# One sigmoid for both score tiles of a visit, fixed PSUM banks in the runs of blocks, and one gate multiplication per block on GpSimd

## The chip, the core and the metric

The kernel runs on one core of one Trainium2 chip. The metric is the device time of one execution in microseconds (us), the median of several runs; lower is better. The engines of the core are named as in the profile: PE is TensorE (matmuls), PEld its weight loads, DVE VectorE, ACT ScalarE, POOL GpSimd, SP SyncE. POOL also issues the loads from device memory, SP the stores. PSUM, into which PE writes, has eight banks of 512 float32 columns on 128 partitions.

## What is computed

Sigmoid attention for 8 batches of 12 heads, then a gated two-layer network on its output, everything in float32 at the borders:

```
scores = q @ k.T / sqrt(64) - log(448)      # q, k, v: (8, 12, 448, 64)
attn   = sigmoid(scores) @ v                # heads side by side: x is (3584, 768)
h      = x @ w_in                           # (3584, 2048)
g      = h * sigmoid(beta * h)              # beta: (2048,)
out    = g @ w_out                          # (3584, 768)
```

## The kernel before

All matmuls take float16 operands and add up in float32 in PSUM. The order of the instructions on every engine is the order in which the Python code issues them; each engine works through its own queue in that order, and semaphores hold it where data or a buffer isn't ready.

**Groups and visits.** Four heads make a group `g`; three groups (QPB = 3) make a batch, so there are 24 groups. The 448 keys of a group are taken in four parts `jt`: three of 128 keys, and a last one of 64 keys. A *visit* `visit(g, jt)` (line 246) computes the scores of one part: eight matmuls (line 222; sixteen in the last part, which a visit does for two groups at once) into two *score tiles* of two PSUM banks each, and then `weigh` (line 233, the sigmoid on ACT at line 236) once for each tile, 128x896 values at a time, into a slot of `attns`. The slots (NAT = 14) are handed out by age from `at_free`. A later visit writes into the same two score tiles, so its matmuls wait until these sigmoids have read them. `attend(g)` (line 281) multiplies the weights of a whole group with v (line 292) into two further banks, and DVE casts these into `xT` (line 301).

**Fill.** Between the scores of two visits PE works on *units* of a list `fill`: single matmuls of the dense layers. First come units of the first layer (line 312, whose gate is a sigmoid on ACT at line 323 and a multiplication on DVE at line 326) and plain units of the second layer (line 341). From about a quarter of the kernel on, the second layer runs as `pairs` of token tiles in Strassen's form: seven products of ND = 8 units each (line 563) on sums of hidden tiles that DVE makes (line 552), with DVE and ACT adding the results up (lines 581 to 586). A product holds a PSUM bank (`held`) until its result is out. `single` (line 379) does a tile that has no partner. The loop at the end of the kernel sets the pace: with the estimates M1_US, M2_US for a unit and AV_US = 1.3 us for an `attend`, it spreads what is left of `fill` evenly over the visits that are left in the phase, and a visit that has an `attend` gets fewer units.

**Banks.** Score tiles have four of the eight banks while visits run (`share_psum(2)`); the other four go to whoever asks (`bank`), the one not held that was used longest ago first.

**Runs of blocks.** Three times (`first_layer`, batches 2 and 3, 4 and 5, 6 and 7) the visits stop, and the first layer of two batches runs as a Strassen product too: `blocks` (line 483), eight blocks `i` of seven products of three matmuls each (`product1`, line 465). A block ends in four results: A and D in banks where they are accumulated, B in its bank, and E, which DVE writes to SBUF (a slot of `attns`, line 525). Each gets its gate: a sigmoid on ACT (line 476) into one of three buffers `sg`, and a multiplication on DVE (line 479). ACT also makes the copies at lines 500 and 503, DVE the addition at line 511. The gates of E, D and B of a block are issued in the next block's round, so a ninth round ends the run. Eight units of `fill` are issued in the first round (two calls of `other()`, four units each) and four in the last round, between the last products 3 and 4. All eight banks serve the run; `bank` picks them by age, and A must get a bank whose last use had 448 columns. After it, `share_psum(2)` takes the four free banks used longest ago, in pairs, for the score tiles.

**Sums of weights.** Strassen's form needs sums of the weights, which DVE makes in halves of 128x1536 (`in_sum`, line 425, `weight_sum`, line 407). `some_sum` issues one after each visit, from visit (4, 2) on: S3, S2, S4, then T7, T6, T1, then T4 and T3 in place in `w_out`, and S1 in place in `w_in` once the first layer of batch 1 is issued.

Of the kernel before, what the change touches and what calls it, by code (L numbers as in the profile page):

```python
# [13 lines left out]
def kernel(  # L14
# [10 lines left out]
    nc = tc.nc  # L25
    AF = mybir.ActivationFunctionType
    ALU = mybir.AluOpType

    B, H, S, D = q.shape
# [11 lines left out]
    QPB = H // HQ  # L41
    NHC = DM // P
    NB1 = DFF // P // 2
# [5 lines left out]
    MSCALE = 1.0 / math.sqrt(D)  # L49
# [14 lines left out]
    used = dict.fromkeys(range(8), 0)  # L64
    scored = []
    held = {}

    psp = ctx.enter_context(tc.tile_pool(name="psp", bufs=1, space=bass.MemoryType.PSUM))
    ps = psp.tile([P, 8, 512], FP32, name="ps")
    n_sc = [0]  # L70
    width = [0] * 8

    def share_psum(sc: int, first: bool = False):

        age = min(used.values()) - 1 if first else max(used.values())
        while len(scored) > sc:
            used.update((i, age) for i in scored.pop())
        while len(scored) < sc:
            free = [i for i in used if i not in held.values()]
            scored.append(  # L80
                min(
                    ((i, i + 1) for i in free if i + 1 in free),
                    key=lambda two: sorted((used[i] for i in two), reverse=True),
                )
            )
            for i in scored[-1]:
                del used[i]

    def touch(i: int):
        used[i] = max(used.values()) + 1  # L90

    def bank(cols: int = S, hold=None, written: int = 0):
        i = min((i for i in used if i not in held.values() and width[i] >= written), key=used.get)
        touch(i)
        if hold is not None:
            held[hold] = i
        width[i] = cols
        return ps[:, i, 0:cols]

    nlogs = const.tile([P, 1], FP32, name="nlogs")  # L100
    dummy = const.tile([P, 1], FP32, name="dummy")
# [3 lines left out]
    NAT = 14  # L105
# [124 lines left out]

    places = {}

    def weigh(sco, n: int, places=()):
        slot = next((i for i in at_free if i in places), at_free[0])
        at_free.remove(slot)
        nc.scalar.activation(  # L236
            out=attns[:, slot, :, 0:n],
            in_=sco[:, :, 0:n],
            func=AF.Sigmoid,
            bias=nlogs[:, 0:1],  # L240
            scale=MSCALE,
        )
        return slot


    def visit(g: int, jt: int, also=()):
        if jt < JF:
            todo = [[s] for s in (2 * g, 2 * g + 1)]
        else:
            todo = [[2 * h, 2 * h + 1] for h in (g, *also)]  # L250
        todo = [(score_tile(), slots) for slots in todo]
        for e in range(PAIR):
            for sco, slots in todo:
                for s in slots:
                    for hh in range(2):
                        score(sco, 0, s, jt, hh, e, 0, S)
        for sco, slots in todo:
            slot = weigh(sco, S, places.get(g, ()))
            for s in slots:
                at_use(slot, (s, jt, 0), slice(0, S))  # L260

# [209 lines left out]
                skip_group_check=not start,  # L471
            )

    def gate(h, dc: int, b: int):
        sg = sigp.tile([P, S], FP32, tag="sg", name="sg")
        nc.scalar.activation(  # L476
            out=sg, in_=h, func=AF.Sigmoid, bias=0.0, scale=beta_sb[:, dc : dc + 1]
        )
        return lambda: nc.vector.tensor_tensor(  # L479
            out=gt[:, dc, b % 2 * S : b % 2 * S + S], in0=h, in1=sg, op=ALU.mult  # L480
        )

    def blocks(b: int, other):

        kept = {}

        def whole(key, i):
            h = kept.pop((i, key))
            if (i, key) in held:
                touch(held.pop((i, key)))  # L490
            half, second = {"A": (0, 0), "D": (0, 1), "B": (1, 0), "E": (1, 1)}[key]
            return gate(h, i + half * NB1, b + second)

        for i in range(NB1 + 1):
            p5 = scratch(6 + i % 2, 1).bitcast(FP32)
            if i < NB1:
                B = kept[i, "B"] = bank(S, (i, "B"))
                product1(b, i, 1, B, True)
                A = kept[i, "A"] = bank(S, (i, "A"), S)
                nc.scalar.copy(out=A, in_=B)  # L500
                D = kept[i, "D"] = bank(S, (i, "D"))
                product1(b, i, 5, D, True)
                nc.scalar.copy(out=p5, in_=D)
            if i:
                product1(b, i - 1, 3, kept[i - 1, "D"], False)
                late = whole("E", i - 1)
            else:
                other()
            if i < NB1:
                product1(b, i, 6, B, False)  # L510
                nc.vector.tensor_tensor(out=D, in0=B, in1=p5, op=ALU.add)  # L511
            if i:
                late()
                whole("D", i - 1)()
            if i < NB1:
                product1(b, i, 2, A, False)
                whole("A", i)()
            if i in (0, NB1):
                other()
            if i:  # L520
                product1(b, i - 1, 4, kept[i - 1, "B"], False)
            if i < NB1:
                product1(b, i, 7, B, False)
                E = kept[i, "E"] = scratch(8 + i % 2, 1).bitcast(FP32)
                nc.vector.tensor_tensor(out=E, in0=B, in1=p5, op=ALU.add)  # L525
# [142 lines left out]
    with tc.manual_schedule():  # L668
# [136 lines left out]
        def first_layer(b: int):  # L805
            while due:
                values(due.pop())
            while soon:
                soon.pop(0)()
            fill_units(len(fill) - at_fill[0] - ND)  # L810
            share_psum(0, True)
            fill.extend(window(b // 2))
            blocks(b, lambda: fill_units(ND // 2))

        for n, (g, jt, also) in enumerate(visits):
            now = lambda g=g, jt=jt, also=also: visit(g, jt, also)
            if jt == 0:
                if g + 2 < NQUAD and g + 2 not in raws:
                    load_qk(g + 2)
                if g + 1 < NQUAD and (g + 1) % QPB == 0:  # L820
                    load_v((g + 1) // QPB)
            if n in turn_at:
                first_layer(turn_at[n])
                share_psum(2)
# [63 lines left out]
```

## Time and profile before

| | |
|---|---|
| time, median of 3 runs (lowest to highest) | 384.84 us (384.68 to 384.84) |
| time of the profiled execution | 385.18 us |
| its span, first to last instruction | 383.4 us |
| PE busy | 374.5 us, 98% of the span |
| ACT busy | 268.4 us, 70% |
| DVE busy | 264.4 us, 69% |
| POOL busy | 67.5 us, 18% |

The span is some 1.8 us shorter than the time of the same execution; changes of the span are taken as changes of the time. The phases that matter: visits with units of the first layer up to about 102 us, visits with Strassen pairs at 104.7 to 133.4, 168.5 to 222.9 and 258.7 to 311.6 us, runs of blocks at 134.5 to 168.5, 224.5 to 258.7 and 313.1 to 347.3 us, and then units alone up to 380 us. A row of a timeline merges neighbours of one kind: start, length until the last of them ends, engine, line, names, count, and in brackets the idle time of the engine before it with what ended that. Matmuls overlap their successors by some 0.07 us in such a row.

### The profile page before, as it was taken

To read this page: it belongs to the slowest core of one execution; us is meant where nothing else is said; L and a number is where in the kernel's file an instruction comes from. 1 tells how busy PE (TensorE), PEld (TensorE's weight loads), DVE (VectorE), ACT (ScalarE), POOL (GpSimd) and SP (SyncE) were. 2 spreads that over 40 slices of the span, in tenths; PEclk is the share of its full clock that TensorE was granted. 3 is DMA by queue.
4 is the path that set the end of the run, shared out by engine and by line. 5 is a ranking of instruction groups with operands and counts; after the bars stand their busy time and mean duration, and the time that the engine had idled before them with its cause. 6 is when DMAs were issued, how large, how long until landed. Compare 5 with 4: busy or idle time off the path is not lost.

```text
span 383.4 us, 7441 instructions
## 1 busy us (share of the span) xinstructions
PE 374.5 (98%) x2927; PEld 187.1 (49%) x2927; DVE 264.4 (69%) x507; ACT 268.4 (70%) x376; POOL 67.5 (18%) x117
## 2 busy tenths in 40 slices
PE   8999999999999999999999999999999999999996
PEld 3467664443344455544444445544444455555663
DVE  3256465779795877886576667888667567889662
ACT  3987877699886758877778748878677747882000
POOL 8833343141141100013214100004100000000000
PEclk9999999999999999999999999999999999999999
DMA  8999999892249330009639431006803031000333
GB/s 116 178 193 203 197 204 199 197 120 50 50 59 192 52 82 0 2 1 120 135 54 212 74 89 41 2 0 91 139 25 84 0 84 41 2 1 3 82 82 125
DMA packets 42403, 34.31 MB, mean 89 GB/s; under 512 B 21872, under 2 KB 38912, under 8 KB 42368
## 3 DMA queue, kind: packets, MB, share of 16 engines
q0 software_dynamic: 36976, 22.81, 43.9%
q1 hardware_dynamic: 5392, 11.02, 9.8%
q8 instruction: 23, 0.38, 0.4%
q14 instruction: 12, 0.10, 0.1%
HBM read 45.62 MB, written 11.01 MB: 148 GB/s over the span
## 4 chain that ended last, share of the span: by engine, by line
PE 90%; DVE 5%; ACT 3%; issue 1%; ACTq 0%; DVEq 0%
PE ps L563 26%; PE ps L465 23%; PE ps L222 12%; PE ps L292 10%; PE ps L312 8%; PE ps L341 4%; PE ps L379 4%; PE ps L682 3%; ACT attns L236 2%; DVE gt L479 2%; DVE ps L511 1%; ACT sg L476 1%; ACT sg L323 1%; DVE gt L326 0%; DVE attns L525 0%
## 5 line engine op out<-in xcount | busy, mean ns | idle before, releaser
L236 ACT ACTIVATE attns<-ps,nlogs 128x896 f16<-128x896 f32 (+1 forms) x171 | 160.5, 991 | 48.1 <-PE ps L222 47.1
L222 PE MATMUL ps<-qT,kT 32*128 32x448 f16 (+3 forms) x864 | 56.6, 340 | 1.7 <-DVE gt L479 0.9
L563 PEld LDWEIGHTS <-sum 128*128 128x128 f16 x440 | 40.4, 98 | 35.7 <-issue 10.4
L476 ACT ACTIVATE sg<-ps,beta_sb 128x448 f32<-128x448 f32 x72 | 45.1, 630 | 7.9 <-PE ps L465 3.8
L465 PE MATMUL ps<-xT,w_S 128*128 128x448 f16 x216 | 48.7, 352 | 0.1
L465 PE MATMUL ps<-xT,w_in 128*128 128x448 f16 x216 | 48.7, 353 | 0.0
L563 PE MATMUL ps<-w_T,sum 128*128 128x384 f16 x264 | 48.7, 327 | 0.0
L301 DVE CAST xT<-ps 128x448 f16<-128x448 f32 (+1 forms) x54 | 28.6, 567 | 28.0 <-PE ps L292 27.7
L131 POOL DMA_DIRECT2D raw<-in_q_dram x27 | 14.9, 551 | 182.9 <-DVE kT L209 172.7
L479 DVE TENSOR_TENSOR gt<-ps,sg 128x448 f16<-128x448 f32 x72 | 42.4, 616 | 0.6 <-ACT sg L476 0.5
L312 PE MATMUL ps<-xT,w_in 128*128 128x224 f16 (+1 forms) x288 | 40.7, 291 | 1.3 <-ACT attns L236 0.8
L292 PE MATMUL ps<-attns,v 128*64 128x448 f16 (+3 forms) x432 | 41.3, 340 | 0.0
L465 PEld LDWEIGHTS <-w_in 128*128 128x128 f16 x288 | 28.0, 98 | 26.6 <-issue 1.1
L581 DVE TENSOR_TENSOR osb<-ps,osb 128x384 f32<-128x384 f32 x55 | 30.5, 554 | 15.1 <-PE ps L563 12.6
L552 DVE TENSOR_TENSOR sum<-gt 128x1024 f16<-128x1024 f16 x55 | 36.4, 680 | 0.2
L563 PE MATMUL ps<-w_out,gt 128*128 128x384 f16 x176 | 33.7, 327 | 0.5 <-DVE w_out L407 0.5
L312 PEld LDWEIGHTS <-w_in 128*128 128x128 f16 x288 | 26.3, 98 | 14.4 <-issue 7.1
L326 DVE TENSOR_TENSOR gt<-ps,sg 128x224 f16<-128x224 f32 (+1 forms) x48 | 21.2, 466 | 17.4 <-ACT sg L323 17.3
L563 PE MATMUL ps<-w_out,sum 128*128 128x384 f16 x176 | 32.3, 327 | 0.7 <-DVE sum L552 0.4
L222 PEld LDWEIGHTS <-kT 32*128 32x128 f16 (+1 forms) x864 | 15.6, 96 | 34.0 <-issue 27.9
L292 PEld LDWEIGHTS <-v 128*64 128x64 f16 (+1 forms) x432 | 18.9, 108 | 24.7 <-issue 17.3
L465 PEld LDWEIGHTS <-w_S 128*128 128x128 f16 x216 | 21.1, 98 | 19.9 <-issue 0.6
(48 smaller groups left out, 350.5 us busy)
## 6 DMA issues: line engine op xcount, KB each, us to landing
out_dram<-osb SPq DMA_DIRECT2D x98, 96.0 KB, 2.4
raw<-in_k_dram POOLq DMA_DIRECT2D x24, 224.0 KB, 5.6
raw<-in_q_dram POOLq DMA_DIRECT2D x21, 224.0 KB, 4.1
v<-in_v_dram POOLq DMA_DIRECT2D x32, 144.0 KB, 6.6
w_in<-in_moe_w_in_dram POOLq DMA_DIRECT2D x8, 384.0 KB, 10.5
w_out<-in_moe_w_out_dram POOLq DMA_DIRECT2D x4, 768.0 KB, 14.0
v<-in_v_dram POOLq DMA_DIRECT2D x16, 48.0 KB, 6.4
out_dram<-osb SPq DMA_DIRECT2D x2, 384.0 KB, 2.4
```

Source lines behind the costliest of these rows:

```text
L222: nc.tensor.matmul(sco[base : base + nk, hh, u0 : u0 + n], kT[g][lo : lo + BLK, jt * P : jt * P + nk, e], qT[g][lo : lo + BLK, c0 : c0 + n ...
L236: nc.scalar.activation(out=attns[:, slot, :, 0:n], in_=sco[:, :, 0:n], func=AF.Sigmoid, bias=nlogs[:, 0:1], scale=MSCALE,)
L292: nc.tensor.matmul(av[hh * D : (hh + 1) * D, 0:n], vs[b][base : base + nk, 2 * (s % NPAIR) + hh, jt], at[base : base + nk, hh, 0:n], start ...
L301: nc.vector.tensor_copy(out=xTs[b][:, s % NPAIR, c0 : c0 + n], in_=av[:, 0:n])
L312: nc.tensor.matmul(m1, w_in16[:, hc, dc * P : (dc + 1) * P], xTs[b][:, hc, c0 : c0 + n], start=(hc == 0), stop=(hc == NHC - 1),)
L326: nc.vector.tensor_tensor(out=gt[:, dc, off : off + n], in0=m1, in1=sg[:, 0:n], op=ALU.mult)
L465: nc.tensor.matmul(out, w[:, c, i * P : (i + 1) * P], m[:, c], start=(start and c == 0), stop=(c == KH - 1), skip_group_check=not start,)
L476: nc.scalar.activation(out=sg, in_=h, func=AF.Sigmoid, bias=0.0, scale=beta_sb[:, dc : dc + 1])
L479: return lambda: nc.vector.tensor_tensor(out=gt[:, dc, b % 2 * S : b % 2 * S + S], in0=h, in1=sg, op=ALU.mult)
L552: nc.vector.tensor_tensor(out=sums[t, i], in0=x, in1=y, op=op)
L563: nc.tensor.matmul(m2, (x if op is None else sums[t, i])[:, dc], w[:, dc], start=first, stop=(dc == ND - 1), skip_group_check=i >= 4,)
L581: nc.vector.tensor_tensor(out=out, in0=in0, in1=in1, op=op)
```

## The change

1. **One sigmoid a visit.** When a visit has two score tiles and the score tiles are banks 0 to 3, `weigh_two` replaces the two calls of `weigh`: one sigmoid over four banks, 128x1792 values, into two neighbouring slots of `attns`, taken as a pair. That is so in 73 visits; 19 sigmoids of 128x896 and the six of 2x224 in the early part stay. `share_psum` always gives the score tiles banks 0 to 3 (0 to 5 at the start).
2. **Fixed banks in a run of blocks.** B and D of block `i` take the pair `i % 3` out of banks 0 and 1, the two remaining "others", and banks 2 and 3; A takes one of two further banks by turns. A bank that a product still holds at the start goes to D of block 1.
3. **E's multiplication on GpSimd.** The gate multiplication of E (it reads SBUF alone) is issued to POOL's queue; those of A, B and D stay on DVE. In the built program an instruction that reloads POOL's library stands ahead of the first one. The gate of the last block's E is issued after all others.
4. **Units at the end of a run.** Instead of four units between the last products 3 and 4, there are two, and six more after the last product 4, ahead of the last E gate and of the next visit. Banks 0 to 3 are given back to the score tiles ahead of these units.
5. **Sums moved.** The sums S3, S2, S4 may start at the first visit with full tiles, (3, 0), and so the T sums move up too; S1 waits until 32 units of the first pairs are issued.
6. **Pace.** AV_US is 1.5 instead of 1.3, and the loop leaves 1.35 us of units instead of 2.0 us ahead of the first two runs. In the built program a visit with Strassen units now has mostly 11 or 12 of them where it had 11, and 2 where it had 3 beside an `attend`.

PE's instructions are the same in number and shape; only their order moves.

```diff
-    def share_psum(sc: int, first: bool = False):
+    def share_psum(sc: int):
+        scored[:] = [(2 * i, 2 * i + 1) for i in range(sc)]
+        last = max(used.values())
+        for i in range(2 * sc):
+            used.pop(i, None)
+        for i in range(2 * sc, 8):
+            used.setdefault(i, last)
...
+    def weigh_two(sco, places):
+        two = [i for i in range(0, NAT, 2) if i in at_free and i + 1 in at_free]
+        slot = min(two, key=lambda i: (i not in places, max(at_free.index(i), at_free.index(i + 1))))
+        at_free.remove(slot)
+        at_free.remove(slot + 1)
+        nc.scalar.activation(
+            out=attns[:, slot : slot + 2].rearrange("p n h s -> p (n h) s"),
+            in_=sco, func=AF.Sigmoid, bias=nlogs[:, 0:1], scale=MSCALE,
+        )
+        return slot, slot + 1
...
     def visit(g: int, jt: int, also=()):
-        for sco, slots in todo:
-            slot = weigh(sco, S, places.get(g, ()))
+        if len(todo) == 2 and len(scored) == 2:
+            ats = weigh_two(ps[:, 0:4, 0:S], places.get(g, ()))
+        else:
+            ats = [weigh(sco, S) for sco, _ in todo]
+        for slot, (_, slots) in zip(ats if n_sc[0] % 2 == 0 or len(todo) == 1 else ats[::-1], todo):
...
-    def gate(h, dc: int, b: int):
+    def gate(h, dc: int, b: int, engine):
-        return lambda: nc.vector.tensor_tensor(
+        return lambda: engine.tensor_tensor(
...
-    def blocks(b: int, other):
+    def blocks(b: int, other, scores: int):
+        rest = sorted(used, key=used.get)
+        firsts = [i for i in rest if width[i] == S and i not in held.values()][:2]
+        others = sorted((i for i in rest if i not in firsts), key=lambda i: i in held.values())
+        (b0, d0), (b2, d2) = scored
+        share_psum(0)
+        def take(key, i):
+            at = firsts[i % 2] if key == "A" else ((b0, d0), others, (b2, d2))[i % 3][key == "D"]
...
         def whole(key, i):
-            return gate(h, i + half * NB1, b + second)
+            return gate(h, i + half * NB1, b + second, nc.gpsimd if key == "E" else nc.vector)
...
             if i:
                 product1(b, i - 1, 3, kept[i - 1, "D"], False)
+            if 0 < i < NB1:
                 late = whole("E", i - 1)
...
-            if i in (0, NB1):
-                other()
+            if i == 0:
+                other(ND // 2)
+            if i == NB1:
+                share_psum(scores)
+                other(2)
             if i:
                 product1(b, i - 1, 4, kept[i - 1, "B"], False)
...
+        other(ND - 2)
+        whole("E", NB1 - 1)()
...
-        sums_todo += [(in_sum, n, p, L1E) for n in ("S1",) for p in range(2)]
+        sums_todo += [(in_sum, n, p, L1E + 4 * ND) for n in ("S1",) for p in range(2)]
...
-                if sums_todo and (g, jt) > (QPB + 1, 1) and at_fill[0] >= sums_todo[0][3]:
+                if sums_todo and at_fill[0] >= sums_todo[0][3] and (sums_todo[0][0] is in_sum or (g, jt) > (QPB + 1, 1)):
...
-        AV_US = 1.3
+        AV_US = 1.5
...
-            todo = left_us(L1B) if g < 2 * QPB else left_us(len(fill)) - (2.0 if g < 6 * QPB else 4.0)
+            todo = left_us(L1B) if g < 2 * QPB else left_us(len(fill)) - (1.35 if g < 6 * QPB else 4.0)
```

More of the change, by code (lines that the diff above doesn't have):

```diff
@@ L71, with bank @@
     width = [0] * 8
-    def share_psum(sc: int, first: bool = False):
[L75 to L87, printed above, removed]
-    def touch(i: int):
[L90 to L94, printed above, removed]
+    def share_psum(sc: int):
[5 more added lines that the diff above has]
+            used.setdefault(i, last)
+    def touch(i: int):
+        used[i] = max(used.values(), default=0) + 1
+    def bank(cols: int = S, hold=None, at=None):
+        if at is None:
+            at = min((i for i in used if i not in held.values()), key=used.get)
+        assert at not in held.values()
+        touch(at)
         if hold is not None:
-            held[hold] = i
-        width[i] = cols
-        return ps[:, i, 0:cols]
+            held[hold] = at
+        width[at] = cols
+        return ps[:, at, 0:cols]
     nlogs = const.tile([P, 1], FP32, name="nlogs")
@@ L231, with weigh @@
     places = {}
-    def weigh(sco, n: int, places=()):
-        slot = next((i for i in at_free if i in places), at_free[0])
-        at_free.remove(slot)
+    def weigh(sco, n: int):
+        slot = at_free.pop(0)
         nc.scalar.activation(
@@ L243, in weigh @@
         return slot
+    def weigh_two(sco, places):
[5 more added lines that the diff above has]
+            out=attns[:, slot : slot + 2].rearrange("p n h s -> p (n h) s"),
+            in_=sco,
+            func=AF.Sigmoid,
+            bias=nlogs[:, 0:1],
+            scale=MSCALE,
+        )
+        return slot, slot + 1
     def visit(g: int, jt: int, also=()):
@@ L496, in blocks @@
             if i < NB1:
-                B = kept[i, "B"] = bank(S, (i, "B"))
+                B = take("B", i)
                 product1(b, i, 1, B, True)
-                A = kept[i, "A"] = bank(S, (i, "A"), S)
+                A = take("A", i)
                 nc.scalar.copy(out=A, in_=B)
-                D = kept[i, "D"] = bank(S, (i, "D"))
+                D = take("D", i)
                 product1(b, i, 5, D, True)
@@ L511, in blocks @@
                 nc.vector.tensor_tensor(out=D, in0=B, in1=p5, op=ALU.add)
+            if 0 < i < NB1:
+                late()
             if i:
-                late()
                 whole("D", i - 1)()
@@ L517, in blocks @@
                 whole("A", i)()
-            if i in (0, NB1):
-                other()
+            if i == 0:
+                other(ND // 2)
+            if i == NB1:
+                share_psum(scores)
+                other(2)
             if i:
@@ L810, in first_layer @@
             fill_units(len(fill) - at_fill[0] - ND)
-            share_psum(0, True)
             fill.extend(window(b // 2))
-            blocks(b, lambda: fill_units(ND // 2))
+            blocks(b, fill_units, 2 if b < B - 2 else 0)
         for n, (g, jt, also) in enumerate(visits):
```

5 lines of the change are left out of this document (3 added, 2 removed).

## The prediction

> **What bounds the kernel now.** I read the page first, then what PE waited for, then stretches of PE's and ACT's timelines.
>
> ```profile
> span 383.4 us, 7441 instructions
> ...
> PE 374.5 (98%) x2927; PEld 187.1 (49%) x2927; DVE 264.4 (69%) x507; ACT 268.4 (70%) x376; POOL 67.5 (18%) x117
> ...
> PE 90%; DVE 5%; ACT 3%; issue 1%; ACTq 0%; DVEq 0%
> ```
>
> PE is busy for 98% and makes 90% of the chain that ended last. PE's instructions stay the same in number and shape, so the time can change only by what PE waits. The waits that the trace lists are short (us in total, times, longest):
>
> ```profile
> PE ps L222 <- DVE gt L479: 0.9, 1, 0.9
> ...
> PE ps L563 <- DVE w_out L407: 0.5, 1, 0.5
> PE ps L563 <- DVE sum L552: 0.4, 1, 0.4
> ```
>
> But a busy PE can hide a wait: a matmul that stands still behind another is drawn within one row. The visits show it; PE first, then ACT:
>
> ```profile
> 61.58 0.60 PE L222 MATMUL ps<-qT,kT 32*64 32x448 f16 x16
> ...
> 185.00 0.57 PE L222 MATMUL ps<-qT,kT 32*128 32x448 f16 x8
> ...
> 187.67 0.57 PE L222 MATMUL ps<-qT,kT 32*128 32x448 f16 x8
> 188.18 1.31 PE L563 MATMUL ps<-w_out,gt 128*128 128x384 f16 x7
> 189.33 0.81 PE L563 MATMUL ps<-w_out,sum 128*128 128x384 f16 x4
> 190.07 0.80 PE L222 MATMUL ps<-qT,kT 32*128 32x448 f16 x8
> ```
>
> ```profile
> 185.61 1.91 ACT L236 ACTIVATE attns<-ps,nlogs 128x896 f16<-128x896 f32 x2 [0.65 <-PE ps L222]
> ...
> 188.34 1.91 ACT L236 ACTIVATE attns<-ps,nlogs 128x896 f16<-128x896 f32 x2 [0.83 <-PE ps L222]
> ```
>
> The same eight score matmuls take 0.57 us or 0.80 us. The long one began 2.40 us after the visit before it, with 11 units between. ACT began 0.67 us after that visit (0.61 us after the one at 185.00), and its two sigmoids ended at 188.34 + 1.91 = 190.25. The visit at 190.07 wants to write the second score tile at once, loses 0.23 us, and so goes on at 190.30, 0.05 us after the sigmoid. So a visit followed by 11 units is bounded by the loop scores, two sigmoids, next scores. How much this takes in all, by the three phases with Strassen pairs (score line alone; stretch, length, PE busy with its matmuls, PEld busy, clock, DMA share, GB/s):
>
> ```profile
> 104.70:133.40 28.70, 7.18 (x96) 1.80 (x96) 1.00 0.64 101
> 168.50:222.90 54.40, 14.25 (x192) 3.60 (x192) 1.00 0.70 113
> 258.70:311.60 52.90, 13.54 (x184) 3.39 (x184) 1.00 0.42 77
> ```
>
> 472 matmuls are 45 visits of 8 and 7 of 16. Clean ones cost 45 x 0.57 + 7 x 0.60 = 29.9 us; PE spent 34.96 us. So 5.1 us of "busy" is standing still.
>
> **The change, part by part.** The sum is made against the profiled execution, 385.18 us; the median of the runs shown, 384.84 us, lies 0.34 us below, and I carry that difference over.
>
> *One sigmoid a visit.* The two lengths that the trace has:
>
> ```profile
> L236 ACT ACTIVATE attns<-ps,nlogs 128x896 f16<-128x896 f32 x165 | 157.4, 1004 | 48.1 <-PE ps L222 47.1
> ...
> L236 ACT ACTIVATE attns<-ps,nlogs 128x448 f16<-128x448 f32 x6 | 3.8, 635 | 0.0
> ```
>
> 448 columns more cost 1004 - 635 = 369 ns, so 1792 columns should take 1004 + 2 x 369 = 1742 ns, against the 1.91 us of the pair. The next scores may start 0.61 to 0.67 + 1.74 + 0.05 = 2.40 to 2.46 us after the last ones, and all four banks come free together, so the first matmul waits, not the third. What PE has in between: 2.40 us with 11 units, 2.56 us with 12 (a unit is 1.15 us / 7 = 0.164 us, from 188.18 to 189.33), and beside an `attend` 185.00 to 187.67 = 2.67 us with 3 units, hence 2.51 us with the 2 that it now gets. Only the visits with 11 units can still wait, by 0 to 0.06 us. By the changed order there are 26 of them; at 0.04 us that is 1.0 us. Of the 5.1 us, 0.74 us belong to the two visits counted next; 4.4 us less 1.0 us, less 0.2 us for the rounding of rows, gives **-3.2 us** (bounds -1.8 with 0.1 us left per visit, and -4.4).
>
> *The visits after a run of blocks.*
>
> ```profile
> 167.08 0.81 PE L563 MATMUL ps<-w_out,gt 128*128 128x384 f16 x4
> 167.89 0.73 PE L465 MATMUL ps<-attns,w_in 128*128 128x448 f16 x3
> 168.55 0.37 PE L222 MATMUL ps<-qT,kT 32*128 32x448 f16 x1
> 169.84 0.57 PE L222 MATMUL ps<-qT,kT 32*128 32x448 f16 x7 [0.93 <-DVE gt L479]
> ...
> 261.12 0.37 PE L222 MATMUL ps<-qT,kT 32*128 32x448 f16 x2
> 261.67 0.57 PE L222 MATMUL ps<-qT,kT 32*128 32x448 f16 x6 [0.17 <-ACT attns L236]
> ```
>
> After the first run the scores stand from 168.55 to 169.84, since the bank still waits for a late gate of the last block: 1.29 us. After the second they lose 0.55 us one visit later, since ACT is late. With fixed banks the last block uses none of banks 0 to 3: their last readers are the gates of block 6, which DVE finishes in the last round, and six more units (1.0 us) now stand before the scores, during which ACT does the last gates. I count both as gone, 1.84 us, and half of the 0.16 us that the last product 4 waits behind the four units in each of three runs (0.81 us for them instead of 4 x 0.164): **-2.1 us** (bounds -1.5 and -2.3). What is late next is the gate of B, wanted by the last unit of the second product, over 1 us later.
>
> *E's multiplication on POOL.* The run of blocks today, by window (length, then PE, PEld, DVE, ACT and POOL busy), then its rows on PE (one block apart), and on ACT, and the group of DVE's multiplication that moves:
>
> ```profile
> 134.50:168.50 34.00, 34.00 (x182) 17.51 (x180) 27.66 (x51) 26.12 (x46) 0.00 (x0) 1.00 0.10 24
> ```
>
> ```profile
> 143.81 1.30 PE L465 MATMUL ps<-xT,w_S 128*128 128x448 f16 x6
> ...
> 147.79 1.30 PE L465 MATMUL ps<-xT,w_S 128*128 128x448 f16 x6
> ```
>
> ```profile
> 143.45 0.52 ACT L500 COPY ps<-ps 128x448 f32<-128x448 f32 x1 [0.32 <-PE ps L465]
> ...
> 144.44 0.67 ACT L476 ACTIVATE sg<-attns,beta_sb 128x448 f32<-128x448 f32 x1
> 145.01 2.09 ACT L476 ACTIVATE sg<-ps,beta_sb 128x448 f32<-128x448 f32 x3
> ```
>
> ```profile
> L479 DVE TENSOR_TENSOR gt<-attns,sg 128x448 f16<-128x448 f32 x24 | 14.8, 617 | 0.8 <-ACT sg L476 0.8
> ```
>
> PE is busy without a gap, a block every 3.98 us; ACT (26.1 of 34 us) and DVE (27.7) have slack, POOL does nothing. So DVE's 0.62 us a block buys nothing inside a run. No row shows POOL multiplying. From below, it should not beat DVE's 0.617 us. From above, its length meets the three `sg` buffers: E, D, A and B take them in turn, so B's sigmoid needs the buffer that POOL reads for E. E's sigmoid ends at 145.11, B's begins at 145.01 + 2.09 - 0.63 = 146.47 (0.63 us being one sigmoid): POOL has 1.36 us, and with ACT's idle 0.32 us about 1.7 us, before a block takes longer. I take **0** and need not choose a value below that. By the Trainium skill (GPSIMD Engine Reference, "Performance versus the Vector engine"), a tensor_tensor add of 2048 columns takes 4497 ns on GpSimd and 2293 ns on VectorE, 1.96 times; from that page I would estimate 1.21 us here, and the sum stays the same; no run so far shows it.
>
> *POOL's queue.* The loads issued behind the multiplications now wait for them.
>
> ```profile
> 128.24 0.54 POOL L131 DMA_DIRECT2D raw<-in_k_dram  x1
> 171.23 0.53 POOL L131 DMA_DIRECT2D raw<-in_q_dram  x1 [42.45 <-DVE kT L209]
> ```
>
> POOL already stands through the run, waiting for DVE's transposes after it. One pair of loads that went early (at 127.72) now goes after the run; its group is transposed six visits (some 15 us) later. **0**, and the reload ahead of the first multiplication has the idle time since 128.8.
>
> *The sums of weights.* T3 now ends long before its product: the 0.5 us on L407 go, **-0.5 us**. In exchange S sums of 0.93 us stand in DVE's queue earlier:
>
> ```profile
> L425 DVE TENSOR_TENSOR w_S<-w_in,w_S 128x1536 f16<-128x1536 f16 x4 | 3.7, 926 | 0.0
> ```
>
> ```profile
> 51.86 0.20 DVE L209 STREAM_TRANSPOSE kT<-raw 128x64 f32<-128x64 f32 x1
> ...
> 53.14 0.57 PE L222 MATMUL ps<-qT,kT 32*128 32x448 f16 x8
> ```
>
> One half comes just before the chain of copies and transposes of which this is the last, whose end (52.06) the scores at 53.14 need. 1.08 us of slack less 0.93 us, less what the gates ahead of it may be late: **+0.4 us** with the `attend` behind it (bounds 0 and 0.93).
>
> *The start and end of a run.* Ahead of the first run six units (1.0 us) less now stand between the last `attend` and product 1, while DVE still makes that product's input sums: **+0.3 us** (0 to 0.6). D of block 1 takes the bank that the last product held: **+0.1 us**. After the last run the wait for the sum on L552 goes, as DVE is 0.6 us ahead: **-0.4 us**.
>
> Sum: -3.2 - 2.1 - 0.5 + 0.4 + 0.3 + 0.1 - 0.4 = -5.4 us; 385.18 - 5.4 - 0.34 = **379.4 us**. With all bounds taken together it reaches from 376.8 to 383.5 us.
>
> **Rivals.**
> 1. *The wait changes its name.* All four banks come free at once, and a slot pair may be late too. If the new sigmoid takes the 1.9 us of the old two, the first matmul of a visit waits as long as the third did: the 3.2 us are gone, 382.6 us, up to 384.0 with the other terms poor. For it: PE needs all four banks, and 11 units leave no slack. Against: the slope of two rows.
> 2. *The first multiplication is late.* If the library is loaded only when the first one starts, ACT stands behind its `sg` buffer, and what it is late beyond 1.7 us is lost, once: 5 us late would give 382.7 us. Against: POOL has 12 us of idle time ahead. By the Trainium skill (GPSIMD Engine Reference, "Instruction dispatch"), the first call after a load of the library pays about 6 us; nothing in this trace shows it.
> 3. *POOL is too slow.* Each us beyond 1.7 us is paid in some 22 blocks. From 2.0 us on the kernel is slower than before: 22 x 0.3 = 6.6 us eat the gain; at 2.5 us it takes 397 us. For it: no row of POOL's arithmetic. Against: that would be over three times DVE's time.
> 4. *POOL and DVE take turns* on SBUF. DVE's five other operations of a block (3 x 616 + 632 + 615 ns, the means of the rows below) make 3.1 us; with t for POOL a block would take 3.1 + t. Beyond t = 0.9 us each block grows; from t = 1.15 us the kernel is slower (22 x 0.28 us), and 1.2 us gives 386.5 us.
>
> ```profile
> L479 DVE TENSOR_TENSOR gt<-ps,sg 128x448 f16<-128x448 f32 x72 | 42.4, 616 | 0.6 <-ACT sg L476 0.5
> ...
> L511 DVE TENSOR_TENSOR ps<-ps,attns 128x448 f32<-128x448 f32 x24 | 15.2, 632 | 16.9 <-PE ps L465 15.4 <-ACT sg L476 1.5
> L525 DVE TENSOR_TENSOR attns<-ps,attns 128x448 f32<-128x448 f32 x24 | 14.8, 615 | 0.0
> ```
>
> Against: these rows read one side from PSUM (`ps`). By the Trainium skill (SBUF — State Buffer, "Who interferes with whom"), a VectorE instruction with two SBUF inputs blocks, and is blocked by, a GpSimd instruction that reads SBUF, for its whole length; one with a single SBUF input isn't. By that rule the turns come only at a run's end, where the last E meets a `sum`, some 0.1 to 0.7 us.
>
> **How the numbers follow.** The sum 0.58; rival 1 0.17; rival 2 0.07; rival 3 0.05; rival 4 0.08; better than all bounds, 0.05. The range 376.8 to 384.0 us holds the first three, 0.82. A measurement can tell about 0.2% from no change, 0.77 us. Faster by more: 0.84 (the sum, rival 2, most of rival 1, the better case). Within: 0.04. Slower by more: 0.12.
>
> **What would show it.** Visits: ACT rows of 1.74 us, score rows of 0.57 us nearly everywhere, PE's time on the score line near 31 us in the three phases. Runs: PE without a gap inside, POOL rows under 1.36 us, no wait of ACT on POOL. Ends: scores that follow six units without a wait on a gate. It would be wrong if PE waits for ACT at most visits, or a block takes more than 3.98 us.

## The result, and the profile after

| | before | after |
|---|---|---|
| median (lowest to highest, runs) | 384.76 us (384.55 to 384.84, 4) | 381.15 us (380.91 to 381.19, 4) |
| profiled execution, its span | 385.18, 383.4 us | 381.19, 379.4 us |

The ratio is 0.9906, 95% interval 0.9889 to 0.9923: 3.6 us faster by the medians, 4.0 us by the two profiled executions, against the 5.4 us of the sum. The page of the changed kernel (span, busy time of each engine, shares of the chain that ended last, and the two groups that are new):

```profile
span 379.4 us, 7379 instructions
...
PE 370.7 (98%) x2927; PEld 186.2 (49%) x2927; DVE 256.8 (68%) x483; ACT 258.4 (68%) x303; POOL 94.7 (25%) x141
...
PE 91%; DVE 5%; ACT 3%; issue 1%; ACTq 0%
...
L245 ACT ACTIVATE attns<-ps,nlogs 128x1792 f16<-128x1792 f32 x73 | 128.0, 1753 | 49.3 <-PE ps L217 49.1
L491 POOL TENSOR_TENSOR gt<-attns,sg 128x448 f16<-128x448 f32 x24 | 27.3, 1137 | 151.3 <-ACT sg L488 151.3
```

The one sigmoid takes 1.753 us (1.742 reckoned) and GpSimd's multiplication 1.137 us. PE still bounds the kernel. The score line in the three phases with Strassen pairs (stretch, length, PE busy with its matmuls):

```profile
104.70:133.00 28.30, 6.35 (x96) 1.62 (x96) 1.00 0.54 86
167.00:222.00 55.00, 12.17 (x192) 3.08 (x192) 1.00 0.73 119
255.50:307.00 51.50, 11.58 (x184) 3.37 (x184) 1.00 0.46 81
```

30.1 us in place of 35.0: the standing still inside the visits is gone. Some of it has only moved. PE's timeline, then ACT's:

```profile
266.30 0.57 PE L217 MATMUL ps<-qT,kT 32*128 32x448 f16 x8
266.81 1.96 PE L593 MATMUL ps<-w_T,sum 128*128 128x384 f16 x11
268.79 0.58 PE L217 MATMUL ps<-qT,kT 32*128 32x448 f16 x8
...
271.22 0.58 PE L217 MATMUL ps<-qT,kT 32*128 32x448 f16 x8
```

```profile
266.99 1.75 ACT L245 ACTIVATE attns<-ps,nlogs 128x1792 f16<-128x1792 f32 x1 [0.82 <-PE ps L217]
269.42 1.75 ACT L245 ACTIVATE attns<-ps,nlogs 128x1792 f16<-128x1792 f32 x1 [0.68 <-PE ps L217]
```

The sigmoid ends at 266.99 + 1.75 = 268.74 and the scores start 0.05 us later, at 268.79. The next ones start at 271.22, which is 269.42 + 1.75 + 0.05. No row shows a wait: PE's rows lie end to end, and the standing still shows only in the distance between starts, which is 2.40 us for 11 units where nothing waits. Over the 25 visits with 11 units and no `attend` (the first at 104.96, the last at 298.71) the score matmul comes 0 to 0.11 us late, 1.5 us in all, and the one visit with ten units (130.53) 0.25 us. In all, 24 of the 52 visits of these phases still come more than 0.02 us late.

The waits that the view of PE's waits lists (total, times, longest) have a new first entry among the products (line 593):

```profile
PE ps L593 <- DVE sum L582: 1.1, 3, 0.8
...
PE ps L593 <- DVE xT L313: 0.4, 1, 0.4
...
PE ps L217 <- DVE kT L200: 0.2, 1, 0.2
```

Before, PE waited for a `sum` once and 0.4 us; now it does three times, each time behind a run of blocks. The timeline of all engines there, first run:

```profile
167.72 0.58 PE L217 MATMUL ps<-qT,kT 32*128 32x448 f16 x8
168.11 1.13 POOL L491 TENSOR_TENSOR gt<-attns,sg 128x448 f16<-128x448 f32 x1 [3.31 <-ACT sg L488]
168.17 1.62 DVE L582 TENSOR_TENSOR sum<-gt 128x1024 f16<-128x1024 f16 x1
168.22 1.47 PE L593 MATMUL ps<-w_out,gt 128*128 128x384 f16 x8
...
169.85 0.66 PE L593 MATMUL ps<-w_out,sum 128*128 128x384 f16 x3 [0.15 <-DVE sum L582]
```

The scores start at 167.72 with no wait on a gate, as forecast. But the `sum` takes 1.62 us where its like takes 0.68, and it ends 0.55 us after POOL's multiplication (168.11 + 1.13 = 169.24). By the distances between matmul starts PE loses 0.31, 0.32 and 0.93 us at the three ends. At the last end PE had stood for a `sum` before too; the rows of the kernel before, then of the changed one:

```profile
349.20 1.90 DVE L552 TENSOR_TENSOR sum<-gt 128x1024 f16<-128x1024 f16 x3
349.95 2.29 PE L563 MATMUL ps<-w_out,sum 128*128 128x384 f16 x13 [0.39 <-DVE sum L552]
```

```profile
344.23 1.13 POOL L491 TENSOR_TENSOR gt<-attns,sg 128x448 f16<-128x448 f32 x1 [3.30 <-ACT sg L488]
344.28 2.82 DVE L582 TENSOR_TENSOR sum<-gt 128x1024 f16<-128x1024 f16 x3
345.96 2.77 PE L593 MATMUL ps<-w_out,sum 128*128 128x384 f16 x16 [0.76 <-DVE sum L582]
```

### The profile page after: what moved, and what is told of

It is laid out like the page before. It is cut to its first block, busy times and chain, and to the rows that moved or that the text cites. A ratio compares the mean times of both kernels' runs of the same rounds, so it can differ in the third digit from the quotient of the medians.

```text
span 379.4 us, 7379 instructions
## 1 busy us (share of the span) xinstructions
PE 370.7 (98%) x2927; PEld 186.2 (49%) x2927; DVE 256.8 (68%) x483; ACT 258.4 (68%) x303; POOL 94.7 (25%) x141
## 4 chain that ended last, share of the span: by engine, by line
PE 91%; DVE 5%; ACT 3%; issue 1%; ACTq 0%
PE ps L477 25%; PE ps L593 25%; PE ps L217 12%; PE ps L304 10%; PE ps L324 9%; PE ps L353 4%; PE ps L391 4%; PE ps L712 3%; DVE sum L582 1%; ACT attns L230 1%; DVE xT L313 1%; ACT sg L488 1%; DVE ps L535 1%; DVE w_S L437 1%; DVE gt L491 1%
## 5 line engine op out<-in xcount | busy, mean ns | idle before, releaser
L245 ACT ACTIVATE attns<-ps,nlogs 128x1792 f16<-128x1792 f32 x73 | 128.0, 1753 | 49.3 <-PE ps L217 49.1
L491 POOL TENSOR_TENSOR gt<-attns,sg 128x448 f16<-128x448 f32 x24 | 27.3, 1137 | 151.3 <-ACT sg L488 151.3
L217 PE MATMUL ps<-qT,kT 32*128 32x448 f16 (+3 forms) x864 | 51.8, 340 | 1.3 <-ACT attns L230 0.6
L491 DVE TENSOR_TENSOR gt<-ps,sg 128x448 f16<-128x448 f32 x72 | 44.6, 619 | 1.4 <-ACT sg L488 1.0
L582 DVE TENSOR_TENSOR sum<-gt 128x1024 f16<-128x1024 f16 x55 | 38.9, 729 | 0.2
L535 DVE TENSOR_TENSOR ps<-ps,attns 128x448 f32<-128x448 f32 x24 | 15.2, 632 | 24.4 <-PE ps L477 24.4
```

The source lines that it names most:

```text
L217: nc.tensor.matmul(sco[base : base + nk, hh, u0 : u0 + n], kT[g][lo : lo + BLK, jt * P : jt * P + nk, e], qT[g][lo : lo + BLK, c0 : c0 + n ...
L245: nc.scalar.activation(out=attns[:, slot : slot + 2].rearrange("p n h s -> p (n h) s"), in_=sco, func=AF.Sigmoid, bias=nlogs[:, 0:1], scal ...
L491: return lambda: engine.tensor_tensor(out=gt[:, dc, b % 2 * S : b % 2 * S + S], in0=h, in1=sg, op=ALU.mult)
L582: nc.vector.tensor_tensor(out=sums[t, i], in0=x, in1=y, op=op)
```

## The experiments

All of them are edits of the changed kernel. Chips differ a little, so each was timed beside the kernel before on its own chip; PE's stalls are read from the profiles.

| kernel | median us | before, same chip | ratio (95% interval) | span |
|---|---|---|---|---|
| lastE_dve | 379.18 | 385.18 | 0.9846 (0.9832 to 0.9859) | 377.9 |
| lastE_early | 379.90 | 385.18 | 0.9865 (0.9851 to 0.9878) | 377.5 |
| allE_dve | 380.55 | 385.18 | 0.9883 (0.9870 to 0.9897) | 378.5 |
| two_sigmoids | 383.42 | 385.18 | 0.9955 (0.9943 to 0.9968) | 381.3 |
| pool_twice | 392.59 | 385.10 | 1.0195 (1.0179 to 1.0210) | 390.7 |
| pool_twice_sg4 | 381.22 | 385.10 | 0.9903 (0.9888 to 0.9918) | 379.5 |
| combo2 | 379.19 | 385.10 | 0.9849 (0.9835 to 0.9864) | 377.4 |
| combo3 | 379.34 | 385.10 | 0.9854 (0.9837 to 0.9870) | 377.6 |
| no_units | 380.81 | 384.87 | 0.9892 (0.9877 to 0.9907) | 379.3 |
| banks_shared | 384.82 | 384.87 | 0.9997 (0.9988 to 1.0006) | 382.7 |
| banks_no_units | 386.99 | 384.87 | 1.0055 (1.0042 to 1.0069) | 385.5 |
| av_13 | 383.58 | 384.87 | 0.9964 (0.9952 to 0.9977) | 381.8 |

**Why the sums are late: lastE_dve and lastE_early.** The theory was that VectorE and GpSimd take turns where both have only SBUF operands; the rival, that the sums are late for another reason.

```diff
-            return gate(h, i + half * NB1, b + second, nc.gpsimd if key == "E" else nc.vector)
+            return gate(h, i + half * NB1, b + second, nc.gpsimd if key == "E" and i < NB1 - 1 else nc.vector)
```

> The changed kernel with the last block's E multiplication of each run on VectorE; the other 21 stay on GpSimd. In the changed kernel the sum behind a run takes 1.62 us instead of 0.68 (168.17) while POOL multiplies (168.11 to 169.24), and PE waits 0.31, 0.32 and 0.93 us for these sums. Theory (VectorE and GpSimd take turns when both have only SBUF operands): the sums take 0.6 to 0.7 us again, all three waits go, 381.15 - 1.5 = 379.6 us. Rival (the sums are late because VectorE is late after the last gates, and 1.62 us is a wait on something else): E's 0.62 us on VectorE make them later still, 381.2 to 382.5 us.

lastE_early keeps the multiplication on GpSimd, earlier:

```diff
-            if 0 < i < NB1:
+            if i:
                 late = whole("E", i - 1)
...
-            if 0 < i < NB1:
+            if i:
                 late()
...
-        whole("E", NB1 - 1)()
```

> The changed kernel with the last E kept on GpSimd but issued as in the other blocks, ahead of D's gate, so that POOL multiplies from about 166.7 to 167.9, before the first sum behind the run. Theory (turns): the sum is short again, though it starts up to 0.6 us later since D's and B's sigmoids stand behind E's; the waits of 0.31 and 0.32 us go and 0.93 falls to about 0.4: 380.0 us. Rival (the sum is slow behind a run whatever POOL does): the sum still takes 1.6 us and starts later, 381.8 to 383 us.

The timeline of lastE_dve, then of lastE_early, behind the first run:

```profile
168.23 0.69 DVE L582 TENSOR_TENSOR sum<-gt 128x1024 f16<-128x1024 f16 x1
...
168.84 0.62 DVE L491 TENSOR_TENSOR gt<-attns,sg 128x448 f16<-128x448 f32 x1
```

```profile
166.08 1.14 POOL L491 TENSOR_TENSOR gt<-attns,sg 128x448 f16<-128x448 f32 x1 [2.06 <-ACT sg L488]
166.56 1.16 DVE L491 TENSOR_TENSOR gt<-ps,sg 128x448 f16<-128x448 f32 x2 [0.79 <-ACT sg L488]
...
167.74 0.69 DVE L581 TENSOR_TENSOR sum<-gt 128x1024 f16<-128x1024 f16 x1
```

In both the `sum` takes 0.69 us. lastE_dve adds E's 0.62 us to VectorE and still loses all three waits; its span is 1.5 us shorter, as expected. lastE_early leaves the work on GpSimd and only ends it before the sums: two of the waits go and the third falls from 0.93 to 0.36 us. So the rival falls: what stretches the `sum` is GpSimd's instruction beside it. VectorE's instructions that read PSUM are not stretched: in the rows of lastE_early the first of two gates starts beside POOL, and both take 1.16 us together; in the runs of blocks of the changed kernel the 21 gates that overlap a multiplication take 0.614 us on average, the others 0.620 us. That is the rule of the Trainium skill that the prediction cited (SBUF — State Buffer, "Who interferes with whom"), and here the traces agree with it on both sides. The sums differ from the gates also in type (f16) and width, which no run separates from the place of their inputs.

**What GpSimd is worth inside a run: allE_dve.**

```diff
-            return gate(h, i + half * NB1, b + second, nc.gpsimd if key == "E" else nc.vector)
+            return gate(h, i + half * NB1, b + second, nc.vector)
```

> The changed kernel with all 24 E multiplications on VectorE. Theory of the prediction (inside a run GpSimd buys nothing, since VectorE has 3.1 + 0.62 = 3.7 of 3.98 us to do in a block): the same time as with only the last E on VectorE, within 0.3 us, and blocks stay at 3.98 us. Rival (VectorE at 93% of a block is late for its gates): blocks grow by up to 0.1 us, 2 us in all, over the kernel with only the last E moved.

It is 1.4 us slower than lastE_dve, so the theory's "within 0.3 us" fell. But no block is longer: from the 13th to the 164th of a run's 168 product matmuls both take 28.56 us. The time is lost at the last block alone, as PE's waits and the timeline of allE_dve show:

```profile
PE ps L477 <- DVE attns L553: 1.0, 3, 0.3
```

```profile
165.07 0.49 PE L593 MATMUL ps<-w_out,gt 128*128 128x384 f16 x2
165.21 0.61 DVE L553 TENSOR_TENSOR attns<-ps,attns 128x448 f32<-128x448 f32 x1
...
165.87 0.73 PE L477 MATMUL ps<-attns,w_in 128*128 128x448 f16 x3 [0.32 <-DVE attns L553]
```

The last product 4 needs the bank that L553 reads; with E's multiplication of the block before ahead of it on VectorE, L553 is late for a product that has only two units before it. From its first product matmul to its last a run takes 33.94 us instead of 33.51: 0.43 x 3 = 1.3 us.

**The price of GpSimd: pool_twice and pool_twice_sg4.**

```diff
-        return lambda: engine.tensor_tensor(
...
+        def multiply():
+            for _ in range(2 if engine is nc.gpsimd else 1):
+                engine.tensor_tensor(
+                    out=gt[:, dc, b % 2 * S : b % 2 * S + S], in0=h, in1=sg, op=ALU.mult
+                )
...
```

> The changed kernel with every E multiplication done twice on GpSimd, into the same place, so 2.27 us a block there instead of 1.14. Theory of the prediction (the third sigmoid after E's needs the sg buffer that POOL reads; 1.36 us are free, 1.7 with ACT's idle time): blocks grow from 3.98 us to about 4.55, ACT waits for POOL, 22 x 0.57 = 12.5 us in the runs, and 3 x 1.1 us more at their ends, where the sums wait for both multiplications: 381.15 + 16 = 397 us. Rival (GpSimd has the whole block, since the slack of the gates takes it up): blocks stay at 3.98 us, only the ends pay, 384.5 us.

pool_twice_sg4 adds:

```diff
-    sigp = ctx.enter_context(tc.tile_pool(name="sigp", bufs=3))
+    sigp = ctx.enter_context(tc.tile_pool(name="sigp", bufs=4))
...
-        still = const.tile([P, 512], FP16, name="still")
+        still = gt[:, NDC - 1, 0:512]
+        beta_in = gt[0:BLK, NDC - 2, 0 : 2 * P].bitcast(FP32)
```

> The same with four sg buffers instead of three (idle weights and the input of beta lie in gt to make room). Theory (the buffer is what bounds, not GpSimd): blocks are back at 3.98 us though POOL works 2.27 us in each, only the ends pay, about 384.5 us. Rival (GpSimd's work itself, or turns with VectorE inside the block, bounds): as slow as with three buffers.

ACT and POOL in pool_twice, and ACT's row among its waits:

```profile
153.10 1.16 ACT L488 ACTIVATE sg<-ps,beta_sb 128x448 f32<-128x448 f32 x2
155.67 0.63 ACT L488 ACTIVATE sg<-ps,beta_sb 128x448 f32<-128x448 f32 x1 [1.42 <-POOL gt L493]
```

```profile
153.28 2.35 POOL L493 TENSOR_TENSOR gt<-attns,sg 128x448 f16<-128x448 f32 x2 [2.20 <-ACT sg L488]
```

```profile
ACT sg L488 <- POOL gt L493: 29.0, 21, 1.4
```

B's sigmoid starts at 155.67, when POOL has ended (153.28 + 2.35 = 155.63). In each run PE stands five times for 0.58 to 0.59 us and once for 0.34: blocks of 4.56 us, against 4.55 reckoned. With a fourth buffer all of that is gone, 381.22 us. So the forecast's limit is the buffer, not the engine. The total came out lower than expected, since six blocks a run pay and not seven, and since the `sum` at each end comes only 0.45 us later than in the changed kernel in pool_twice and no later in pool_twice_sg4, where 1.1 us had been expected in both (a later product of the last end loses 0.23 us in both). POOL and VectorE of pool_twice_sg4 (its lines shift a little):

```profile
167.79 2.67 POOL L492 TENSOR_TENSOR gt<-attns,sg 128x448 f16<-128x448 f32 x2 [2.14 <-ACT sg L487]
```

```profile
167.85 1.62 DVE L585 TENSOR_TENSOR sum<-gt 128x1024 f16<-128x1024 f16 x1
```

The `sum` still takes 1.62 us: it goes between the two multiplications, and these take 2.67 us in place of 2.35. Here turns are taken by instruction, at each of the three ends.

**The visits: two_sigmoids and av_13.** two_sigmoids weighs each tile by itself again, on the same banks and slots:

```diff
-            ats = weigh_two(ps[:, 0:4, 0:S], places.get(g, ()))
+            two = [i for i in range(0, NAT, 2) if i in at_free and i + 1 in at_free]
...
+            ats = [weigh(sco, S) for sco, _ in (todo if n_sc[0] % 2 == 0 else todo)]
...
-        for slot, (_, slots) in zip(ats if n_sc[0] % 2 == 0 or len(todo) == 1 else ats[::-1], todo):
+        for slot, (_, slots) in zip(ats, todo):
```

> The changed kernel with two sigmoids of 896 columns a visit again, on the same banks and slots. Theory (loop of scores, sigmoid, next scores): sigmoids take 2 x 1.0 us less overlap, 1.91 us instead of 1.75, the visits' waits rise from some 1.8 us to about 4.1 us, 383.5 us (1 to 5 us more than 381.15). Rival 1 of the prediction (the wait only changed its name): 381.2 us within 0.5.

It costs 1.9 us by the spans and 2.3 us by the medians (383.42 against 381.15 us), and the standing still is back inside the visits: 3.9 us there, where the changed kernel has 1.8 us ahead of them. Its timeline, PE then ACT:

```profile
277.55 0.78 PE L217 MATMUL ps<-qT,kT 32*128 32x448 f16 x8
```

```profile
275.81 1.91 ACT L230 ACTIVATE attns<-ps,nlogs 128x896 f16<-128x896 f32 x2 [0.70 <-PE ps L217]
```

The theory holds, and rival 1 of the prediction falls, though it is right in part: of the old 4.1 us, 1.8 only changed their place.

```diff
-        AV_US = 1.5
+        AV_US = 1.3
```

> The changed kernel with an attend reckoned at 1.3 us as before instead of 1.5. Visits beside an attend get 3 units again and others 11 instead of 12, some 10. Theory (the loop of 2.49 us bounds every visit of 11 units, 2.40 us, and every one of 10, 2.24 us, while 3 units beside an attend leave 0.2 us unused): the visits wait 1.0 to 1.5 us more, 382.4 us. Rival (the units are the same in number, so it matters little where they stand): 381.15 us within 0.3.

2.4 us slower by the span, twice the theory's. In the three phases 31 visits now have 11 units and five have ten, and those of ten lose 0.25 us each, four of them new; with the further visits of 11 units the visits wait 1.3 us more, as the theory said. The rest it had not seen: 0.99 us at 52.01, where a product of the second layer waits for its gate, less the 0.26 us that stood at that place, and 0.45 us at 292.65, where an `attend` comes just before a product that opens a bank.

**The scores after a run: no_units, banks_shared, banks_no_units.** All three have lastE_dve's edit. no_units takes away the eight units; banks_shared puts B and D of the last block into score banks; banks_no_units does both:

```diff
-                other(2)
...
-        other(ND - 2)
```

```diff
-            at = firsts[i % 2] if key == "A" else ((b0, d0), others, (b2, d2))[i % 3][key == "D"]
+            at = firsts[i % 2] if key == "A" else ((b0, d0), others, (b2, d2))[2 if i == NB1 - 1 else i % 3][key == "D"]
...
+        share_psum(scores)
         other(ND - 2)
```

> The changed kernel with the last E of each run on VectorE (379.2 us), and without the eight units of the second layer between the last block's products and the next scores; the units go to the later visits. Theory (the fixed banks alone took away the wait of the scores on a gate; the units only gave ACT time): the first scores after a run start at once, with no wait on a gate, and the second visit waits 0.5 to 0.7 us since ACT's first sigmoid stands behind those of B and E; in exchange 16 visits get 12 units instead of 11 and wait 0.09 us less: about 379 us, within 0.8. Rival (the units are what covers the gates): the first scores wait about 1.3 us as in the kernel before, 381 to 382 us.

> The changed kernel with the last E of each run on VectorE, and with B and D of the last block in two of the four score banks (2 and 3) instead of in two others; the eight units stay. Theory: the third score matmul after a run waits for B's gate, which ends 0.42 us after these scores start (168.19 against 167.77): 0.45 us in each of two runs, 380.1 us. Rival (six units are cover enough): no wait, 379.2 us.

> Both together: B and D of the last block in score banks, and no units between them and the scores. Theory (the fixed banks and the units each cover the gates; without both it is the wait of the kernel before): the first visit after a run stands 1.2 to 1.5 us until B's gate, twice, 2 to 3 us more than without the units alone. Rival: as the kernel without the units.

PE after the first run in no_units, in banks_shared and in banks_no_units:

```profile
166.26 0.73 PE L477 MATMUL ps<-attns,w_in 128*128 128x448 f16 x3 [0.22 <-DVE attns L552]
166.92 0.57 PE L217 MATMUL ps<-qT,kT 32*128 32x448 f16 x8
167.43 2.12 PE L591 MATMUL ps<-w_out,gt 128*128 128x384 f16 x12
169.91 0.58 PE L217 MATMUL ps<-qT,kT 32*128 32x448 f16 x8 [0.36 <-ACT attns L245]
```

```profile
169.11 0.57 PE L217 MATMUL ps<-qT,kT 32*128 32x448 f16 x8 [0.41 <-DVE gt L491]
```

```profile
169.60 0.58 PE L217 MATMUL ps<-qT,kT 32*128 32x448 f16 x8 [1.38 <-DVE gt L491]
```

Without units but with fixed banks the scores start at once; with units but shared banks they lose 0.47 us by the distance of starts, against 0.45 reckoned; without both, 1.45 us, near the old wait of 1.29 us. So the fixed banks remove the wait on a gate, and the units give ACT its time: without them the second visit waits 0.43 us after each of the first two runs, and the last product 4 stands 0.38 us in all three, 2.0 us in all. That is why no_units, at 380.81 us, lies above the theory's 379 us within 0.8: the theory had left out product 4. banks_shared and banks_no_units lose 1.48 us a run more, 4.4 us of their totals of 384.8 and 387.0 us. That was not expected and is the edit's own: block 7 now wants a bank that block 5's gate still reads (PE waits for that gate from 160.42), two blocks apart instead of three.

**Two of the smaller stalls: combo2 and combo3.** combo2 is lastE_dve with the sum of weights behind the transposes in the visit that ends quad 3:

```diff
+            if (g, jt) == (QPB, JF):
+                double_v_last(1)
+                transpose(g + 1, 0)
+                transpose(g + 1, 1)
             some_sum()
             for f in soon[:2]:
                 f()
             del soon[:2]
-            if (g, jt) == (QPB, JF):
-                double_v_last(1)
-                transpose(g + 1, 0)
-                transpose(g + 1, 1)
```

> The changed kernel with the last E of each run on VectorE and, in the visit that ends quad 3, the sum of weights behind the transposes of the next quad instead of ahead of them. Theory (the scores after that visit wait 0.26 us since the sum of 0.93 us stands ahead of kT in VectorE's queue): that wait goes, 0.26 us less than with only the last E moved, 378.9 us. Rival (kT waits for its load, so the place of the sum does not matter): the same time as with only the last E moved.

combo3 is combo2 with another pace:

```diff
-        AV_US = 1.5
+        AV_US = 1.6
...
-            todo = left_us(L1B) if g < 2 * QPB else left_us(len(fill)) - (1.35 if g < 6 * QPB else 4.0)
+            todo = left_us(L1B) if g < 2 * QPB else left_us(len(fill)) - (1.7 if g < 6 * QPB else 4.0)
```

> The same as the kernel before it in this list with another pace: 1.6 us instead of 1.5 reckoned for an attend, and 1.7 instead of 1.35 us left over at the end of a phase, so that one visit with ten units and an attend right ahead of a product that opens a bank go. Theory (11 units and two matmul lines make 2.40 us against a loop of 2.49, 12 units 2.56): the visits wait about 0.2 us less, and the stalls of 0.62 us (202) and 0.25 us (130) go: 378 us, 0.5 to 1.0 less than without it. Rival (these stalls move to other visits): the same time within 0.3.

In combo2 the wait of 0.26 us for kT is gone, but the `attend` behind it now stands 0.15 us, and the median is that of lastE_dve, so what is left cannot be measured. combo3's theory fell: the stalls at 130 (0.25 us) and 202 (0.62 us) stayed, and the visits' small waits moved to others. lastE_dve, combo2 and combo3, which their intervals do not tell apart, are the fastest versions, 1.5% under the kernel before.

## Why the prediction was right, and where its sum was off

Direction and causes were right; the sum was 1.4 us too good between the two profiled executions, and 1.75 us against the median, since the 0.34 us that the prediction carried over did not recur. The bounds that it states term by term, taken together, give some 377.2 to 383.2 us (a term without bounds put at nothing where that widens the range) and not 376.8 to 383.5; the measured 381.15 us lies inside both. By its steps, with the losses read from distances between matmul starts in the two profiled executions:

- **One sigmoid a visit, -3.2: about -2.35.** 4.1 us inside the visits went and 1.8 us came back ahead of them. The mechanism, the length of the sigmoid and the 11-unit visits as the ones that can still wait were right. The size was off: ACT starts 0.63 or 0.69 us after the scores (269.42 after 268.79, 266.99 after 266.30), so the loop takes 2.43 or 2.49 us and not 2.40 to 2.46; a visit of 11 units waits 0.06 us on average and not 0.04, and the one visit of ten units was left out.
- **The visits after runs and product 4, -2.1: -2.15.** Both waits are gone, 1.84 us, and the three stalls of 0.16 us fell to 0.05 us. The shared-bank kernels show why: the banks remove the gate's wait, the units ACT's. That product 4, behind two units in place of four, lost no more is GpSimd's doing (allE_dve).
- **E's multiplication on GpSimd, 0: right inside a run, wrong at its ends.** A block keeps its 3.98 us. At the last block the move saves 1.3 us, which the prediction did not see, and behind the run it costs 1.5 us; the two nearly cancel. The step that failed is the last one of rival 4, which named this very place and "0.1 to 0.7 us" and then left it out of the sum. That the saving was there to meet it is luck.
- **The end of the last run, -0.4: +0.2.** This is the term with the wrong sign, and by that cause: VectorE is indeed ahead, its sums start 1.71 us after the run's last product matmul (344.28, 342.57) where they had started after 2.09 us (349.20, 347.11), but the first `sum` stands behind POOL's multiplication, and PE loses 0.93 us instead of 0.70.
- **The two earlier ends, not in the sum: +0.6.** The same cause.
- **T3 -0.5: -0.7**, read from the profiles; no run tests it alone. **Sums of S +0.4: +0.26**, at the place and by the chain named. **Start of the first run +0.3: +0.24**, at the third product (136.76). **Block 1's bank +0.1: 0.** POOL's queue and the loads: 0, as said.
- **Not foreseen: +0.2 and -0.25.** An `attend` just before a product that opens a bank costs 0.62 us at 202 where one at 125 had cost 0.44. Two waits of units before 55 us shrink by 0.14 and 0.11 us.

Together -2.35 - 2.15 + 0.2 + 0.6 - 0.7 + 0.26 + 0.24 + 0.2 - 0.25 = -3.95 us, beside the 4.0 us between the spans.

Rivals: the wait changed its name for 1.8 of 4.1 us only. The first multiplication was not late: E's sigmoid ends at 139.09 + 0.67 = 139.76 and POOL's row starts at 139.84 and lasts 1.13 us:

```profile
139.84 1.13 POOL L491 TENSOR_TENSOR gt<-attns,sg 128x448 f16<-128x448 f32 x1 [21.56 <-ACT sg L488]
```

The Trainium skill's price of some 6 us for a first call (GPSIMD Engine Reference, "Instruction dispatch") does not appear here; POOL had been idle for 21.56 us before, so no run shows whether it was paid in that time. GpSimd was not too slow, and pool_twice confirms the limit of 1.7 us by its price beyond it. The turns with VectorE came only where both have SBUF operands alone, at the ends of the runs, and not inside the blocks as rival 4 priced them.

## What to carry to other kernels

A busy engine at 98% can still lose microseconds that no wait shows: compare the distance of equal groups of instructions, and after a change look for the loss ahead of the group as well as inside it. Moving work to an idle engine is priced at the places where its neighbours change, the first and last block of a run, and not in its middle; and the instruction to fear on GpSimd is the one that runs while VectorE needs two SBUF operands.

## What the runs showed of the hardware

- A VectorE add with two SBUF inputs that starts beside a GpSimd multiplication ends about 0.55 us after it (1.62 us in place of 0.69), while VectorE's gates with one PSUM input are not stretched (0.61 us). Between two GpSimd instructions VectorE gets its turn, and the second of them is delayed (2.67 us for two in place of 2.35).
- GpSimd's multiplication of 128 x 448 (f32 inputs, f16 output) takes 1.137 us beside VectorE's 0.617, 1.84 times as long; the Trainium skill's pair of figures (GPSIMD Engine Reference, "Performance versus the Vector engine") gives 1.96 for an add of 2048 columns, 6% more. The measured ratio holds for this shape.
